# Eight wide warm-up products of TensorE become 32 narrow ones

## The chip, the cores and the metric

The kernel runs on one core of a Trainium2 chip. A core has five engines with instruction streams of their own: TensorE (PE in the profile; PEld is its weight load), VectorE (DVE), ScalarE (ACT), GpSimd (POOL) and SyncE (SP), which here only issues transfers. Engines wait for each other by semaphores. The metric is the device time of one execution in microseconds (us); the median of several runs counts.

## The reference

The kernel computes an attention that picks chunks of keys, then a feed-forward block with a gate. There are 4 sequences with 8 heads, 768 tokens and head size 64. For each query, every chunk of 32 keys gets an upper bound of its score from the chunk's smallest and largest key values; the 6 best chunks (causal) are kept, and softmax attention is done over them alone. The result, 3072 tokens by 512, goes through an RMS norm and the feed-forward block of width 1536.

```python
ub = np.sum(np.maximum(q[:, :, :, None, :] * k_min[:, :, None, :, :],
                       q[:, :, :, None, :] * k_max[:, :, None, :, :]), axis=-1)
...
top_chunks = np.argsort(ub, axis=-1)[..., -top_k:]
scores = scale * np.matmul(q, k.transpose(0, 1, 3, 2))
...
g = xn @ w_gate
silu = g * (1.0 / (1.0 + np.exp(-g)))
val = xn @ w_val
return (silu * val @ w_out).astype(np.float32)
```

## The kernel before

The work is cut into 12 blocks of 256 tokens (a sequence and one of its three parts), in the order of the list `ORDER`. For each block and each group of four heads, DVE transposes keys and queries and reduces the keys to their extremes; TensorE makes the bounds (`upper_first`, line 540, in fp32 for the first part of a sequence; `upper`, line 522, for the others); DVE turns the bounds (tile `ubn`, line 565), takes the best six with a max instruction and makes a mask in two layouts (tiles `mtd` and `mto`, lines 591 and 597). TensorE then makes the scores (line 760) and adds the mask to them in the same accumulation with a product against `chunkrow` (line 771). ACT takes the exponential (tile `pt`, line 810), POOL cuts the triangle on the diagonal, and TensorE multiplies by the values (line 836). After the norm, the feed-forward products stand in line 960 (gate and value) and line 1008 (output); `tanh`, `tg` (line 971), `vs` and `hh` lie between them on ACT, DVE and POOL. Scores go to PSUM tiles called `S`, everything else that TensorE writes to tiles called `F`.

No planner runs at build time. `Plan.STEPS` is a written list: a number from 0 up means operation `x // 8` on engine `x % 8`, and the instructions of each engine stand in the order of this list. `Plan.SLOTS` gives the buffers. A negative number is a step without a result that anyone reads: warm-up products of the identity matrix with itself, written to one of the four `F` tiles, to keep TensorE at work while it waits. `run` (line 227) reads such a number, and `keep_busy` (line 1072) emits the products:

```python
n, slot = divmod(-x, 16)
fill[-1](n // 2, slot, n % 2)
```

So the lowest bit of `n` says whether the products are wide (512 columns, four copies of the identity side by side) or narrow (128 columns), and the rest is their number. Each product has a weight load of its own ahead of it. The first warm-up products of the kernel are 84 narrow ones (the numbers -2368 and -320) while the first transfers are under way; all later ones of before are wide, 38 in all.

In TensorE's program an fp32 product (lines 522 and 540) becomes two loads and two products, every other product one load and one product. With branches and the semaphore waits that stand alone, the program of before has about 9,533 instructions. TensorE's code lies in memory and comes to the engine through a transfer queue of its own during the run.

The two places that the change touches lie early. The first four wide products stand between the scores of the first block's first head group and the bounds of its second (line 540); the second four between the scores of the second head group and the next scores with their mask (lines 760 and 771).

Of the kernel before, what the change touches and what calls it, by code (L numbers as in the profile page):

```python
# [33 lines left out]
class Plan:  # L34
# [13 lines left out]
        131, 228, 233, 123, 155, 3, 99, 249, 244, 27, 257, 276, 291, 34, 281, 268, 299, 83, 412,  # L48
        425, 203, 67, 107, 75, 433, 420, 538, 115, 139, 315, 466, 323, 473, 482, 380, 396, 443, 490,
        545, 42, 498, 404, 307, 522, 388, 529, 506, 594, 515, 179, 611, 562, -2368, -320, 616, 601,  # L50
        554, 672, 626, 681, 571, 50, 457, 578, 786, 587, 634, 689, -82, -82, 792, 642, 57, 650, 699,
        848, 802, 9, 810, 857, 818, 658, 865, 826, 834, 665, 1098, 875, 841, -144, 704, 451, -80,
        736, 912, 713, 746, 922, 754, 1107, 721, 930, 1185, -82, -114, 880, 19, 1042, 731, 331,
        1114, 1049, 1058, 889, 1066, 897, 1130, 1660, 1075, 961, -402, -114, 1248, 1170, 1628, 760,
        1257, 1644, 1082, 1091, 907, 195, 971, 1177, 936, 1684, -80, 1192, 1676, 1362, 977, 1138,
# [1051 lines left out]
```

## Time and profile before

| | |
|---|---|
| median of 3 runs | 293.87 us (292.45 to 294.37) |
| profiled execution | 291.88 us, of which the span is 290.1 us |
| instructions recorded in the span | 11444 |
| busy: TensorE, DVE, ACT, POOL | 96%, 75%, 71%, 58% |
| instruction transfers, queue q8 | 37 packets, 0.61 MB |
| HBM | 28.58 MB read, 6.29 MB written |

Times in the profile count from the start of the span. A busy share is an average over the whole span. "Idle before" names what ended an idle time as far as the profile can tell; "issue" stands where it shows nothing that the engine waited for. Where the engine named had been done long before, something else was waited for. A few records of products are missing (4714 of 4742); the weight loads are complete. The ends of products are modelled, since they overlap.

### The profile page before, as it was taken

Reading aid. Unit: us, or ns where it says so; the run is one execution under the profiler, and the core shown is the slowest. Engines: PE = TensorE matmul, PEld = TensorE weight load, DVE = VectorE, ACT = ScalarE, POOL = GpSimd, SP = SyncE. Lnnn points to the kernel's source line nnn. Section 1 sums busy time; section 2 is a strip of 40 time slices with the busy share of each in tenths; the row PEclk is TensorE's granted clock in tenths of the full one; section 3 lists DMA queues with packets and bytes.
Section 4 is the critical chain, followed back from the end, with each engine's and each line's share of the span. In section 5 each row is a group of like instructions: output and inputs, shape, how many; then the busy total and the mean of one; then the engine's idle time right before and its main releaser. Section 6 shows DMA issues by size and latency. Waiting matters only on the chain.

```text
span 290.1 us, 11444 instructions
## 1 busy us (share of the span) xinstructions
PE 279.4 (96%) x4714; PEld 215.3 (74%) x4742; DVE 216.6 (75%) x626; ACT 206.8 (71%) x355; POOL 167.9 (58%) x268
## 2 busy tenths in 40 slices
PE   7999899999999899999999999999999999999995
PEld 7647897668877667888676787688678966688763
DVE  3878878889898799799989999987573724374341
ACT  2976787678888898877876595877679767564421
POOL 9668779979988785567684485517224207112420
PEclk9999999999999999999999999999999999999999
DMA  9999999989599684468699815912013200303022
GB/s 178 219 194 225 204 211 119 150 160 127 113 165 156 144 155 88 112 99 158 112 178 143 150 25 98 121 12 75 2 20 93 21 3 2 111 18 58 0 91 92
DMA packets 86388, 31.94 MB, mean 110 GB/s; under 512 B 74816, under 2 KB 81728, under 8 KB 86336
## 3 DMA queue, kind: packets, MB, share of 16 engines
q1 hardware_dynamic: 55616, 22.56, 34.0%
q0 software_dynamic: 29712, 7.87, 27.0%
q10 hardware_dynamic: 1008, 0.79, 1.5%
q8 instruction: 37, 0.61, 0.9%
q14 instruction: 15, 0.12, 0.1%
HBM read 28.58 MB, written 6.29 MB: 120 GB/s over the span
## 4 chain that ended last, share of the span: by engine, by line
PE 92%; DVE 3%; issue 2%; DMA 1%; ACT 1%; ACTq 0%; DVEq 0%
PE F L960 44%; PE F L1008 21%; PE S L760 8%; PE F L836 8%; PE S L771 3%; PE F L522 3%; PE F L1075 2%; PE F L540 1%; DMA kraw<-in_k_dram 1%; DVE kx L651 1%; PE F L916 1%; DVE qT L636 0%; DVE kT L636 0%; ACT pt L810 0%; DVE tg L971 0%
## 5 line engine op out<-in xcount | busy, mean ns | idle before, releaser
L810 ACT ACTIVATE pt<-S 128x1024 bf16<-128x1024 f32 (+3 forms) x104 | 85.5, 857 | 29.5 <-PE S L771 26.3
L982 POOL TENSOR_TENSOR hh<-tg,vs 128x512 bf16<-128x512 bf16 x48 | 55.6, 1167 | 45.2 <-DVE tg L971 28.3
L960 PE MATMUL F<-xsT,wg 128*128 128x256 bf16 (+1 forms) x640 | 72.4, 262 | 0.5 <-issue 0.5
L960 PE MATMUL F<-xsT,wv 128*128 128x256 bf16 (+1 forms) x640 | 71.6, 262 | 0.1
L1008 PE MATMUL F<-wo,hh 128*128 128x512 bf16 (+1 forms) x272 | 65.5, 370 | 1.8 <-issue 0.6
L971 DVE SCALAR_TENSOR_TENSOR tg<-th,F 128x512 bf16<-128x512 bf16 x72 | 48.4, 679 | 25.1 <-ACT th L967 19.9
L960 PEld LDWEIGHTS <-wg 128*128 128x128 bf16 x640 | 56.1, 98 | 9.4 <-issue 1.0
L960 PEld LDWEIGHTS <-wv 128*128 128x128 bf16 x640 | 56.1, 98 | 7.7 <-issue 0.2
L967 ACT ACTIVATE th<-F 128x512 bf16<-128x512 f32 x72 | 42.6, 599 | 14.4 <-PE F L960 13.1
L780 POOL TENSOR_SCALAR_AFFINE_SELECT pt<-pt 128x512 bf16<-128x512 bf16 x48 | 31.8, 669 | 27.5 <-ACT pt L810 27.4
L1008 PEld LDWEIGHTS <-hh 128*128 128x128 bf16 x300 | 27.6, 98 | 25.2 <-issue 0.4
L979 ACT ACTIVATE vs<-F 128x512 bf16<-128x512 f32 x48 | 28.5, 599 | 8.9 <-PE F L960 6.0
L760 PE MATMUL S<-qb,kb 32*128 32x256 bf16 (+1 forms) x800 | 33.1, 253 | 0.3 <-issue 0.2
L651 DVE TENSOR_REDUCE kx<-kT 128x16 f32<-128x512 f32 x48 | 31.1, 670 | 0.2
L836 PEld LDWEIGHTS <-pt 128*128 128x128 bf16 x672 | 25.4, 98 | 4.8 <-issue 1.4
L836 PE MATMUL F<-VX,pt 128*128 128x65 bf16 x672 | 27.5, 194 | 1.3 <-issue 1.1
L975 DVE TENSOR_TENSOR hh<-tg,F 128x512 bf16<-128x512 bf16 x24 | 16.1, 682 | 10.2 <-PE F L960 10.0
L760 PEld LDWEIGHTS <-kb 32*128 32x128 bf16 x800 | 13.6, 92 | 13.3 <-issue 11.9
L376 POOL DMA_DIRECT2D VX<-in_v_dram x24 | 22.9, 956 | 0.0
L771 PE MATMUL S<-mto,chunkrow 32*128 32x128 bf16 (+2 forms) x384 | 20.0, 203 | 1.1 <-DVE tg L971 1.0
L771 PE MATMUL S<-mtd,chunkrow 32*128 32x128 bf16 (+2 forms) x384 | 20.3, 203 | 0.0
L771 PEld LDWEIGHTS <-chunkrow 32*128 32x128 bf16 x768 | 18.6, 93 | 2.2 <-issue 1.3
(73 smaller groups left out, 341.2 us busy)
## 6 DMA issues: line engine op xcount, KB each, us to landing
out_dram<-osb SPq DMA_DIRECT2D x23, 256.0 KB, 3.4
kraw<-in_k_dram SPq DMA_DIRECT2D x72, 64.0 KB, 3.3
qraw<-in_q_dram SPq DMA_DIRECT2D x72, 64.0 KB, 3.0
VX<-in_v_dram POOLq DMA_DIRECT2D x24, 128.0 KB, 4.8
QX<-qT SPq DMA_DIRECT2D x32, 64.0 KB, 2.2
wv<-in_moe_w_val_dram POOLq DMA_DIRECT2D x3, 512.0 KB, 11.0
wg<-in_moe_w_gate_dram POOLq DMA_DIRECT2D x3, 512.0 KB, 12.7
wo<-in_moe_w_out_dram POOLq DMA_DIRECT2D x3, 512.0 KB, 9.9
```

Source lines behind the costliest of these rows:

```text
L651: plan.op(f"ext{n}{J}", "DVE", 0.585, 0.67, lambda n=n, op=op: VE.tensor_reduce(out=at(kx)[:, g, n], in_=at(kT).rearrange("p h (j c x) -> ...
L760: TE.matmul(s[a // 2][:, a % 2, c0:c0 + q1 - q0], kbt[r, t, ks], qbt[r, t, q0:q1], start=(t == 0), stop=(t == 1 and not mask), skip_group_ ...
L771: TE.matmul(o, chunkrow[r, BLK * kg + P * e:BLK * kg + P * (e + 1)], mv, start=False, stop=(d == 1), skip_group_check=True)
L780: GE.affine_select(out=d, in_=d, compare_op=ALU.is_ge, fill=0.0, base=0, pattern=[[0, 4], [1, P]], channel_multiplier=-1)
L810: lambda pt=pt, hs=hs, c0=c0, c1=c1, x=sc[hp]: SE.activation(out=at(pt)[:, hs, c0:c1], in_=at(x)[:, :, c0:c1], func=ACT.Exp, scale=SCALE), ...
L836: TE.matmul(o[:, a, :], p_[:, a, off:off + P], vt[:, e, 4 * g + a, :], start=(kb_ == 0 and a == 0), stop=(kb_ == nkb - 1 and a == 3), skip ...
L960: TE.matmul(at(p_)[:, n * W:(n + 1) * W], w[:, g, ht * P:(ht + 1) * P], at(xT)[:, g, x0:x0 + W], start=(g == 0), stop=(g == NP - 1), skip_ ...
L967: plan.op(f"tanh{U}.{hp}", "ACT", 0.48, 0.6, lambda th=th, gp=gp: SE.activation(out=at(th), in_=at(gp), func=ACT.Tanh, scale=0.5), pri - 0 ...
L971: VE.scalar_tensor_tensor(out=at(tg), in0=at(th), scalar=1.0, in1=at(gp), op0=ALU.add, op1=ALU.mult), pri - 30, reads=[th, gp], writes=[tg ...
L979: plan.op(f"vcopy{U}.{hp}", "ACT", 0.48, 0.6, lambda vs=vs, vp=vp: SE.activation(out=at(vs), in_=at(vp), func=ACT.Copy), pri + 0.1, reads= ...
L982: plan.op(f"hh{U}.{hp}", "POOL", 1.11, 1.16, lambda tg=tg, vs=vs, hh=hh: GE.tensor_tensor(out=at(hh), in0=at(tg), in1=at(vs), op=ALU.mult) ...
L1008: TE.matmul(at(op)[:, cs], at(key)[:, o:o + P], wo[:, ht, cs], start=(ht == 0), stop=(ht == NHT - 1), skip_group_check=True)
```

## The change

In `STEPS` two numbers -82 (each two wide products into `F` tile 2) become one number -514 (16 narrow products into the same tile), and -144 (four wide products into `F` tile 0) becomes -512 (16 narrow ones into the same tile). The columns that pass through TensorE are the same: 4 × 512 and 16 × 128. There are 24 more weight loads and 24 more products in TensorE's program, 24 instructions at each place, 48 in all. Everything that stands behind them in the program lies 48 instructions further on. The programs of the other engines are unchanged.

```diff
@@ -48,8 +48,8 @@
         131, 228, 233, 123, 155, 3, 99, 249, 244, 27, 257, 276, 291, 34, 281, 268, 299, 83, 412,
         425, 203, 67, 107, 75, 433, 420, 538, 115, 139, 315, 466, 323, 473, 482, 380, 396, 443, 490,
         545, 42, 498, 404, 307, 522, 388, 529, 506, 594, 515, 179, 611, 562, -2368, -320, 616, 601,
-        554, 672, 626, 681, 571, 50, 457, 578, 786, 587, 634, 689, -82, -82, 792, 642, 57, 650, 699,
-        848, 802, 9, 810, 857, 818, 658, 865, 826, 834, 665, 1098, 875, 841, -144, 704, 451, -80,
+        554, 672, 626, 681, 571, 50, 457, 578, 786, 587, 634, 689, -514, 792, 642, 57, 650, 699,
+        848, 802, 9, 810, 857, 818, 658, 865, 826, 834, 665, 1098, 875, 841, -512, 704, 451, -80,
         736, 912, 713, 746, 922, 754, 1107, 721, 930, 1185, -82, -114, 880, 19, 1042, 731, 331,
```

## The prediction

> **What bounds the kernel now.** I read the page first, then TensorE's waits, then the timeline around the warm-up products, then a table of windows that counts instructions up to chosen moments, and last the instruction queue. From the page:
>
> ```profile
> PE 279.4 (96%) x4714; PEld 215.3 (74%) x4742; DVE 216.6 (75%) x626; ACT 206.8 (71%) x355; POOL 167.9 (58%) x268
> ...
> q8 instruction: 37, 0.61, 0.9%
> ...
> PE 92%; DVE 3%; issue 2%; DMA 1%; ACT 1%; ACTq 0%; DVEq 0%
> ```
>
> TensorE (PE) is busy for 96% of the span and makes up 92% of the chain that ended last. So a time by which it falls behind is lost unless an idle stretch further on gives it back. Its waits:
>
> ```profile
> PE F L836 <- issue: 1.1, 1, 1.1
> PE S L771 <- DVE tg L971: 1.0, 1, 1.0
> PE F L1008 <- issue: 0.6, 4, 0.2
> PE F L960 <- issue: 0.5, 1, 0.5
> PE F L1075 <- DVE ubn L565: 0.3, 1, 0.3
> PE S L760 <- issue: 0.2, 1, 0.2
> ```
>
> Apart from the start these are all of them, 3.7 us. Four (1.1, 1.0, 0.5 and the last 0.2) sit inside groups of like instructions; three of them by the timeline, and a row of DVE:
>
> ```profile
> 15.96 0.28 PE L760 MATMUL S<-qb,kb 32*128 32x128 bf16 x5 [0.20 <-issue]
> ...
> 26.79 0.44 DVE L597 STREAM_TRANSPOSE mto<-mk 64x32 bf16<-64x32 bf16 x2
> ...
> 29.61 0.20 PE L771 MATMUL S<-mto,chunkrow 32*128 32x32 bf16 x4 [1.01 <-DVE tg L971]
> ...
> 99.13 0.70 PE L836 MATMUL F<-VX,pt 128*128 128x65 bf16 x17 [1.10 <-issue]
> ```
>
> The second is put down to DVE's tg, but it reads mto, which DVE had written by 27.23 (26.79 + 0.44), so DVE isn't what it waits for. The idle is counted from the modelled end of the product before; from start to start each is about 0.2 us longer, the length of a short record: 0.4, 1.2, 0.7 (at 36) and 1.3. The windows say where the four lie in the instruction stream (columns: window, length, then busy time and count of PE, PEld, DVE, ACT, POOL, clock, DMA share, GB/s):
>
> ```profile
> 0.00:9.46 9.46, 7.39 (x96) 7.29 (x96) 4.68 (x11) 4.23 (x4) 8.52 (x27) 1.00 1.10 175
> 0.00:13.46 13.46, 11.33 (x195) 9.52 (x199) 8.47 (x30) 8.06 (x14) 10.35 (x32) 1.00 1.12 194
> 0.00:15.90 15.90, 13.63 (x222) 10.63 (x222) 9.83 (x34) 9.80 (x18) 12.79 (x35) 1.00 1.14 199
> 0.00:27.47 27.47, 24.84 (x452) 18.20 (x453) 19.57 (x69) 17.60 (x34) 20.23 (x52) 1.00 1.25 209
> 0.00:29.50 29.50, 25.98 (x477) 19.09 (x477) 21.44 (x74) 19.63 (x38) 22.27 (x55) 1.00 1.22 204
> 0.00:34.31 34.31, 30.68 (x580) 23.64 (x581) 24.96 (x80) 23.21 (x46) 25.45 (x60) 1.00 1.23 204
> 0.00:36.20 36.20, 32.25 (x605) 25.04 (x605) 26.71 (x84) 24.70 (x49) 27.32 (x62) 1.00 1.23 204
> 0.00:41.10 41.10, 36.99 (x706) 29.68 (x706) 31.16 (x91) 28.54 (x56) 30.60 (x70) 1.00 1.23 204
> 0.00:42.35 42.35, 38.24 (x731) 30.89 (x732) 31.98 (x94) 29.79 (x57) 31.85 (x71) 1.00 1.23 205
> 0.00:93.95 93.95, 89.34 (x1483) 69.29 (x1493) 77.07 (x226) 71.50 (x137) 78.01 (x141) 1.00 1.05 171
> 0.00:97.07 97.07, 92.41 (x1586) 71.63 (x1598) 79.86 (x246) 74.58 (x142) 80.48 (x144) 1.00 1.04 171
> 0.00:99.00 99.00, 93.37 (x1613) 72.38 (x1622) 81.35 (x253) 76.45 (x144) 81.46 (x145) 1.00 1.03 170
> ```
>
> Each weight load has one product, so the position is twice the PEld count and the few branches and semaphore waits that the program holds by then (3, 6, 8, 11 or 23). At the four waits it is 222×2+6 = 450, 477×2+8 = 962, 605×2+8 = 1218, 1622×2+23 = 3267: after the first by 512, 768 and 2817, that is, 256 apart to one instruction. They are limits of code blocks, and the whole stream (about 9,533) over the 37 instruction packets gives 258 each. Single packets, by the DMA view of short windows (13.3:13.5, 26.7:26.9, 96.4:96.6):
>
> ```profile
> q8 instruction: 1, 0.02, 34.0%
> q8 instruction: 1, 0.02, 41.8%
> q8 instruction: 1, 0.02, 40.8%
> ```
>
> The first took 34.0% of 16 engines over 0.2 us, 1.09 us, and TensorE resumed at 15.96, 2.6 us after the packet's start; the other two resumed 2.8 and 2.6 us after. The limit before the first stands at 194, which TensorE passed at 9.46 (96×2+3 = 195): so a block seems to be asked for when TensorE enters the one before it, and to start some 4 us later while the DMA share is 1.1 to 1.25. So before 42 us the kernel is held back by its own code, one block per 6 to 7 us.
>
> **The change part by part.** The products themselves:
>
> ```profile
> 7.59 1.78 PE L1075 MATMUL F<-ident 128*128 128x128 bf16 x29
> ...
> 16.38 3.41 PE L1075 MATMUL F<-ident 128*128 128x512 bf16 x15
> ...
> L1075 PE MATMUL F<-ident x122: 219/314/390, 2.1 to 33.7; 128*128 128x128 bf16 x84, 128*128 128x512 bf16 x38
> ```
>
> A row's time holds one record's tail, 0.22 us for a narrow and 0.39 for a wide product. So a narrow one takes (1.78 − 0.22)/28 = 0.056 us and a wide one (3.41 − 0.39)/14 = 0.216. Removed are 8 × 0.216 = 1.73 us, added 32 × 0.056 = 1.78: **+0.06 us**. Their 24 additional weight loads run beside the products, as in the row of 29. Nothing moves on another engine, no wait is added and no DMA.
>
> What moves is the code limits. Both places stand after instruction 194 and before 450, so the limits up to 194 stay, and every later one (450, 706, ...) falls on work that was 48 instructions earlier: 402, 658, 914, 1170, 1426, ..., 3218 of before.
>
> *Limit 450.* The block is asked for at instruction 194, ahead of the change, so its packet starts at 13.3 to 13.5 as now and TensorE can go on at 15.96. It gets to the 402 of before at 13.46 (199×2+6 = 404), now 13.52, and stands for 15.96 − 13.52 = **2.44 us** where it lost 0.4. From there 48 instructions of work, 2.1 us with its seven wide warm-up products, are still to be done that were behind it: it is 15.96 − 13.46 − 0.4 = 2.1 us late. None of this is cover for another wait: DVE and ACT wait for TensorE soon after, and warm-up products are a fixed list that a late TensorE still executes.
>
> *Limit 706* (658): no idle now, and TensorE comes 2.1 us later to it, so none.
>
> *Limit 962* (914). TensorE comes at 27.47 + 2.1 = 29.6. If the packet starts in 26.7:26.9 as now, the block is there at 29.6: the 1.2 us of idle there (28.4 to 29.6) is gone but for 0.1. But instruction 657 of before waits for DVE's ubn (the row of 0.3 us), and the block is asked for at 658, now right behind that wait, which itself comes 2.1 us later; then I count up to 0.8 us. *Limit 1218* (1170): TensorE comes at 34.31 + 2.1 − 1.2 + (0.1 to 0.8) = 35.3 to 36.0, the block at 36.36 + (0 to 0.8), so 1.1 us where 0.7 is lost now. *Limit 1474* (1426): now TensorE shows no wait there, and by the same count it and the block come within 0.1 of each other; I take 0.1 now and then.
>
> The early sum: 0.06 + 2.44 + (0.1 to 0.8) + 1.1 + 0.1 = 3.8 to 4.5, less 0.4 + 1.2 + 0.7 + 0.1 = 2.4 now: +1.4 to +2.1. From the other side: as long as the blocks set the pace, they come at the same times and TensorE is 48 instructions short at each; at 1474 that is the time from 41.10 to 42.35, 1.2 us. So +1.2 to +2.1; I take **+1.8**, near the upper end, since the wait for ubn is a row and stands where the request does.
>
> *Limit 3266* (3218). It costs 1.3 us now. TensorE passes the limit before it, 3010 (1493×2+23 = 3009), at 93.95, and the packet starts at 96.4:96.6, late for this part, behind a load of SP:
>
> ```profile
> 93.25 0.40 SPq L376 DMA_DIRECT2D gB<-in_moe_rms_g_dram  x1
> ```
>
> With the limit at 2962 the request goes out sooner; I can't read from the trace how far ahead of the products the sequencer asks. The quick instructions between 2962 and 3010 take 0.4 us, and the slower products of L960 before them up to 2 us for the same count; so the request is 0.4 to 2 us sooner, an estimate. TensorE needs the block 99.13 − 97.07 less the idle of 1.3 = 0.8 us sooner. So the idle becomes 0.1 to 1.7; if the packet's start does not move at all, 2.1. An earlier request also comes ahead of the 256 KB of gB. I take 0.4, near the lower end for that, which is **−0.9**, with −1.3 and +0.8 as ends.
>
> *The 32 other limits* show no such row (the longest issue wait left is 0.2 us); I take 0, with +0.8 as an end, one new idle of the middle size.
>
> Sum: 1.8 − 0.9 + 0 = **+0.9 us**. The profiled execution took 291.88 us (span 290.1), so 292.8 of its kind; it lies 2.0 under the median of the runs, 293.87, which gives **294.8 us**.
>
> The Trainium skill ("Runtime: NRT & Kernel Launch", Instruction fetch mechanics) has blocks of 256 instructions fetched by the sequencer itself, and calls the cost of crossing a limit mostly hidden. The trace agrees with the 256 and not, in this kernel, with the second; by it alone the sum would be the 0.06 us of the products.
>
> **The rivals.** *Not slower: the late limit pays for the early ones.* The request for 3218 gets ahead of gB and its idle goes but for 0.1 (−1.2), while the request for 914 isn't held by ubn and the early debt is the 1.2 of limit 1474: 0.0, so 293.9. It decides from an early debt below what 3266 gives back. For it: 1.2 us is the bound that the pace gives. Against it: the ubn row.
>
> *The limits don't matter.* The waits would be something else and the products alone count: 293.9. Against it are four idle times that lie 256 apart to the instruction, one of them, at 99.13, ahead of the last 17 of a run of L836 products.
>
> *No gain at 3266.* The packet waits out the same transfers: +0.8 instead of −0.9, with +2.1 early: +2.9, 296.8, and 297.6 with one new idle of 0.8.
>
> *The clock falls.* The first products ran slowly:
>
> ```profile
> 2.07 5.19 PE L1075 MATMUL F<-ident 128*128 128x128 bf16 x47 [2.07 <-POOL ident masks.py:199]
> ```
>
> That is 0.11 us each against 0.056 later: half speed for some 5 us. If an idle of 2.4 us sends TensorE back to it for as long, half of 5.2 is lost: +2.6 on the 0.9, 297.4. Against it: idles of 1.2 us left every window at 1.00 clock. The Trainium skill ("TensorE: Matmul & The Clock Gate", The HAM clock gate) asks for an idle window of about 3.4 us before the clock is halved; 2.4 is below it, and no run shown here has one so long.
>
> **How the numbers follow.** My forecast, early debt with part of it given back, 0.58; late limit pays for all 0.18; limits don't matter 0.03; no gain at 3266 0.15; clock 0.06. About 1% (2.9 us) is what a measurement of this kernel can tell from no change. The forecast and the first two rivals stay within it, but for 0.05 each way for a gap of the early fetches that opens or closes more than I count; the last two lie at or over it. So faster 0.05, same 0.75, slower 0.20. The range goes from the early debt 1.2, 3266 at −1.3 and the runs' own spread below the median (293.87 − 292.45 = 1.4) to the third rival with an idle more: 292.5 to 297.5.
>
> **What would show it.** TensorE idle from about 13.5 to 16 in a group of L771 with an issue wait of some 2.4 us: the central step. Then the DVE tg wait of 1.0 us at 29.6 gone or smaller and moved to the start of an L960 group; an idle near 36 of about 1.1; the issue wait at 98 smaller or gone; all counted positions of these waits again at 450 + 256k. The clock in 15:25 stays 1.00. I'm wrong if the first packet starts sooner than 13.3, if early limits show idles whose sum isn't 3.8 to 4.5, or if a late limit opens a new one.

## The result and the profile after

The kernel after the change took 293.84 us (median; 292.52 to 295.97) beside 292.51 us for the kernel before in the same session, a ratio of 1.0048 with a 95% interval of 1.0027 to 1.0069. It is 1.3 us slower: less than the 1% that the prediction took as the least that counts as a change, but clear of no difference, since the interval doesn't reach 1. The forecast had been +0.9. In absolute terms it had been 294.8 us, 1.0 too high, because it started from a median of three runs (293.87) that lies 1.4 above the one of 22 here, while the difference itself was 0.4 too small.

The execution of after that was profiled is one of its slowest (295.97 us, span 294.2). From its page:

```profile
PE 281.5 (96%) x4738; PEld 216.9 (74%) x4766; DVE 216.9 (74%) x626; ACT 206.7 (70%) x355; POOL 167.8 (57%) x268
...
PEclk9979999999999999999999999999999999999999
...
q8 instruction: 37, 0.61, 0.9%
```

There are 24 more weight loads and still 37 instruction packets. New is the 7 in the third slice of the clock row: TensorE did not have its full clock all the time. TensorE's waits (us in total, times, longest), without the wait for ident at the start and one of 0.3 us for ubn that before has too:

```profile
PE S L771 <- issue: 2.0, 1, 2.0
PE F L960 <- DMA xsT<-xs: 0.9, 1, 0.9
PE F L836 <- DVE tg L971: 0.8, 1, 0.8
PE F L1008 <- issue: 0.6, 4, 0.2
PE F L960 <- DVE tg L971: 0.4, 1, 0.4
PE F L836 <- DVE hh L975: 0.4, 1, 0.4
PE F L540 <- DVE BO L676: 0.4, 1, 0.4
```

Of before's four waits at block limits (0.2, 1.0, 0.5 and 1.1 us) none is left. In their place stands one, larger and early. Five rows are of waits that before did not have: one for BO, early, and four for xsT, tg (two) and hh, all after 113 us. The timeline around the large one:

```profile
14.46 0.18 PE L771 MATMUL S<-mtd,chunkrow 32*128 32x32 bf16 x2
16.59 0.19 PE L771 MATMUL S<-mtd,chunkrow 32*128 32x32 bf16 x2 [1.95 <-issue]
...
17.48 2.33 PE L1075 MATMUL F<-ident 128*128 128x512 bf16 x5
```

TensorE stops after the second of four products of a group, at instruction 450 of its program, which is where the prediction put it. Between the starts of the weight loads on its two sides the idle is 2.18 us, against 0.42 before. The last row is what was not forecast: five wide products take 2.33 us, where in before fifteen took 3.41 us, 0.216 each. The table of windows (window, length, then busy time and count of PE, PEld, DVE, ACT, POOL, granted clock, DMA share, GB/s) has the clock beside it:

```profile
17.36:20.77 3.41, 3.41 (x46) 1.47 (x43) 3.24 (x8) 2.21 (x5) 1.36 (x2) 0.50 1.57 195
13.95:17.36 3.41, 1.42 (x42) 0.91 (x41) 0.85 (x2) 1.28 (x6) 2.48 (x4) 1.00 1.36 217
```

For 3.41 us the clock is 0.50, and in the 3.41 us ahead of that TensorE was busy for only 1.42.

I followed where the time went by matching the weight loads of the two profiled executions in order and taking the difference of their starts. After is 3.1 us behind at the work of before's 13.46 (of it 2.2 at the limit; 0.9 came in ahead of it, with the data of the first products), 4.2 behind at 19.7, within the slow stretch, 2.7 at 29.6, 2.0 at 36.4, 0.9 at 99.1: the idles of before at limits 962, 1218 and 3266, which are missing here, give back 1.2, 0.7 and 1.2. Then it loses again: 1.9 behind at 113.5, 3.6 at 129.4, and 4.1 at the end. This execution lies 2.1 us above the median of its kernel and that of before 0.6 below its own; so the profiles differ by three times what the medians do, and more profiles were needed.

### The profile page after: what moved, and what is told of

Its sections match the earlier page's. It is cut to its first block, busy times and chain, and to the rows that moved or that the text cites. A ratio compares the mean times of both kernels' runs of the same rounds, so it can differ in the third digit from the quotient of the medians.

```text
span 294.2 us, 11492 instructions
## 1 busy us (share of the span) xinstructions
PE 281.5 (96%) x4738; PEld 216.9 (74%) x4766; DVE 216.9 (74%) x626; ACT 206.7 (70%) x355; POOL 167.8 (57%) x268
## 4 chain that ended last, share of the span: by engine, by line
PE 80%; DMA 7%; DVE 5%; SPq 3%; issue 3%; ACT 1%; ACTq 0%; DVEq 0%
PE F L960 39%; PE F L1008 17%; PE S L760 7%; PE F L836 6%; PE F L1075 3%; DMA qraw<-in_q_dram 3%; SPq L376 3%; PE S L771 2%; PE F L522 2%; PE F L540 1%; DMA out_dram<-osb 1%; DMA kraw<-in_k_dram 1%; DMA xsT<-xs 1%; DVE xs L890 1%; DVE qT L636 1%
## 5 line engine op out<-in xcount | busy, mean ns | idle before, releaser
L780 POOL TENSOR_SCALAR_AFFINE_SELECT pt<-pt 128x512 bf16<-128x512 bf16 x48 | 31.1, 654 | 29.4 <-ACT pt L810 29.1
L1075 PE MATMUL F<-ident 128*128 128x128 bf16 (+1 forms) x146 | 18.4, 292 | 2.4 <-POOL ident masks.py:199 2.1
```

The costliest lines, as they stand in the source:

```text
L780: GE.affine_select(out=d, in_=d, compare_op=ALU.is_ge, fill=0.0, base=0, pattern=[[0, 4], [1, P]], channel_multiplier=-1)
```

## The experiments

Times are medians beside the kernel before in the same session, with the ratio and its 95% interval. "From start to start" is the idle of a limit measured between the starts of the weight loads on its two sides, so that a limit without idle has about 0.05. The position of a limit is named by its instruction in TensorE's program (450, 706, 962, ...).

**1. The first of the two places alone**, a shift of 24 instead of 48.

```diff
- ... 634, 689, -82, -82, 792, 642, ...
+ ... 634, 689, -514, 792, 642, ...
```

> Only the first of the two places is changed: four wide products become 16 narrow ones, and the code limits from 450 on fall on work that stood 24 instructions earlier (426, 682, 938, 1194, ..., 3242 of before). Theory of the limits: the first idle lies between the one of before (0.4 us) and the one of the changed kernel (2.2 us), about 1.7 us, ends near 16, and stands at instruction 450 of the program; the idle at 3266 shrinks from 1.3 to about 0.8. Rival (narrow products cost by themselves): half of what the whole change costs, +0.7 us, and the waits where they were before. Theory of the clock: an idle of 1.7 us halves TensorE's clock in fewer executions than one of 2.2 us.

293.69 us beside 292.64, ratio 1.0036 (1.0003 to 1.0069). The idle at 450 is 1.67 us from start to start, as the halved shift asks. That the size fits so well is partly luck, since both sides of it were late in this execution: the packet started at 14.62 instead of 13.38, and TensorE was 1.3 us late on its way to the limit, 0.9 of it in a wait for BO. The idle has moved to another group, 24 instructions of work from where 48 put it:

```profile
15.72 0.29 PE L836 MATMUL F<-VX,pt 128*128 128x65 bf16 x4
17.47 0.30 PE L836 MATMUL F<-VX,pt 128*128 128x65 bf16 x4 [1.45 <-POOL mhalf L394]
```

It is put down to POOL's mhalf here and to "issue" in after: the name changes with the group, the position in the program doesn't. At 3266 0.27 us is left of 1.29 (I had expected 0.8). The clock is 0.50 from 17.72 to 21.13 here too; of the 12 executions 2 have a mean clock below 0.9965, against 9 of 22 of after. So the second set of narrow products is not needed for the idle, and its place goes with the position of the limit.

**2. The limits put back**: after, with 32 of the narrow products of the kernel's start made eight wide ones. The changed places stay narrow, 48 instructions fewer stand ahead of instruction 194, and all limits from 450 on fall on the same work as before.

```diff
- ... 562, -2368, -320, 616, ...
+ ... 562, -1344, -272, -320, 616, ...
```

> The change as it is, and 32 of the 84 narrow products at the start become 8 wide ones, which takes the 48 instructions out again ahead of limit 194. The limits from 450 on fall on the same work as before the change; the limit at 194 falls on work that stood 48 instructions later. Theory of the limits: idle times again at the places of before (962: 1.2, 1218: 0.7, 3266: 1.3 us). If the block of 450 is asked for when TensorE enters 194, the first idle is 0.8 to 2.0 us instead of 0.4, since 194 is entered 1.6 us later; if it is asked for at a fixed time, 0.4. Rival (the narrow products cost by themselves): the time of the changed kernel, +1.3 us, with the waits of before.

292.84 us beside 292.64, ratio 1.0005 (0.9979 to 1.0030): the loss is gone with the narrow products still in place. The waits of before are back, as at 962:

```profile
29.53 0.18 PE L771 MATMUL S<-mtd,chunkrow 32*128 32x32 bf16 x4
30.61 0.19 PE L771 MATMUL S<-mto,chunkrow 32*128 32x32 bf16 x4 [0.89 <-DVE tg L971]
```

From start to start 1.11 us at 962, 1.06 at 3266. So narrow products in those two places cost nothing by themselves. This run can't tell the limits from a cost of every instruction in the program, since it has as many narrow products in all as before; experiment 3 comes back to that. Two details missed: no idle at 1218 (0.7 expected), and one of 0.09 at 450 where I had expected 0.8 to 2.0. Limit 194 was passed 1.4 us later than in before, but the packet for 450 started only 0.6 us later (14.02 instead of 13.38). So the packet is not simply a fixed time behind the passing of the limit ahead of it: over the thirteen profiles the packet for 450 started 3.0 to 4.4 us behind it.

**3. A wide start**, in before: all 84 narrow products of the start become 21 wide ones, 126 instructions fewer ahead of limit 194.

```diff
- ... 562, -2368, -320, 616, ...
+ ... 562, -592, -112, 616, ...
```

> Before, with all 84 narrow products of the start as 21 wide ones: 126 instructions fewer, the two later places as before. The limits move the other way: 450 falls on work of instruction 576 of before, and is asked for later. Theory of the limits: no idle at 450 at all (needed at 19.9, there at about 18), one of about 1.4 us at the third limit near 30, none or little after; 1.5 us less idle than before, 291.0 us. Rival (the first products or the sum of columns decide): as before, since the columns are the same.

291.20 us beside 292.64, ratio 0.9954 (0.9919 to 0.9989). Its waits hold no limit at all any more:

```profile
PE F L960 <- DVE tg L971: 0.4, 1, 0.4
PE F L960 <- DMA xsT<-xs: 0.3, 1, 0.3
PE F L1075 <- DVE ubn L565: 0.3, 1, 0.3
PE F L836 <- DVE ubn L565: 0.2, 1, 0.2
```

I had expected 1.4 us at the limit near 30, so that detail missed. Along the shared work TensorE is 1.6 us ahead of before at 29.6, 3.5 at 99 and 2.4 at the end.

The medians of all experiments rise with the number of instructions (126 fewer, 78 fewer, as many, 24 more, 48 more), so a small cost of every instruction would fit them nearly as well as the limits. The traces speak against it. Such a cost would show where the instructions are, at the start; but TensorE is only 0.1 us ahead at 19.7. Its lead comes in steps at the places of before's waits, 1.2 us at 962, 0.7 at 1218 and 1.3 at 3266, and stays within 0.2 us between these steps.

**4. The same wide start in after.**

> The changed kernel with the same wide start: 78 instructions fewer than before. Theory of the limits: no idle at 450, one of about 0.9 us near 30, 1.7 us less idle than before, 290.8 us, although the 32 narrow products of the change are all there; and the clock stays at full in all executions, since no idle reaches 2 us. Rival (the narrow products cost by themselves): 1.3 us over the run with the wide start alone.

292.25 us beside 292.64, ratio 0.9984 (0.9949 to 1.0020). I had expected 290.8 us, so this one missed. There is no idle at 450, as expected, but at 962 it is 1.6 us where I had expected 0.9:

```profile
29.40 0.26 PE L836 MATMUL F<-VX,pt 128*128 128x65 bf16 x3
31.04 0.34 PE L836 MATMUL F<-VX,pt 128*128 128x65 bf16 x5 [1.38 <-issue]
```

With 78 instructions fewer instead of 126 the limits fall less well. Beside experiment 3 (292.25 and 291.20 in the same session) the change costs about 1.0 us here too, but the two intervals overlap, so this is not clear of noise. I had also expected a full clock in every execution, since no idle reaches 2 us. But 4 of 12 have a mean clock below 0.9965, as do 4 of 12 in experiment 3, whose profile shows no idle at a limit.

**5. After once more**, for a second profile.

> The changed kernel once more, for a profile in which TensorE's clock is not halved and for the share of executions in which it is. Theory of the clock: the idle of 2 us at 450 is there in each execution; where the clock stays full, the run is about 293.3 us, 0.6 over before, and TensorE's delay at 36 us (work of instruction 1218) is about 0.2 to 1 us instead of 2.0. Rival (the clock has no part in it): the same delays as in the profile with the halved clock.

293.83 us beside 292.36, ratio 1.0050 (1.0015 to 1.0085): the difference holds. The second profile is unlike the first. Here data came late, and TensorE waited for them ahead of limit 450; the row of waits, and the windows around it:

```profile
PE F L540 <- DVE BO L676: 1.5, 1, 1.5
...
8.00:10.00 2.00, 0.49 (x15) 0.32 (x12) 0.95 (x3) 0.59 (x2) 1.01 (x4) 1.00 1.44 191
...
11.98:15.39 3.41, 3.41 (x61) 2.84 (x58) 2.91 (x16) 2.79 (x10) 1.86 (x4) 0.50 1.18 258
```

The clock fell to a half for 3.41 us after that wait, before the limit was reached. TensorE came to 450 late for both reasons and stood only 0.86 us; 0.41 at 962, 0.62 at 1218, none at 3266. It is 1.3 us behind before at 36.4, 0.2 at 99 and 1.4 at the end. In 8 of the 10 executions the mean clock is below 0.9965; their median is 293.90 us, that of the two others 293.18.

**6. The late limits alone**: in before, 8 of the 15 wide products at 16.4 become 32 narrow, so that limits 194 and 450 stay and those from 706 on shift by 48. If the early idle at 450 is the loss and 3266 the gain, this version has the gain alone.

```diff
- ... 1075, 961, -402, -114, 1248, ...
+ ... 1075, 961, -242, -1026, 1248, ...
```

> Before, with the first two places as they were; of the 15 wide warm-up products at 16.4 us eight become 32 narrow ones. The same 48 instructions more, but after limit 450: the first limit stays where it was, all from 706 on shift as in the changed kernel. Theory of the limits: the idle at 450 is 0.4 us as before, the one at 3266 is gone, those at 962 and 1218 come to about 2.3 us together (1.9 before); 0.7 us less idle than before, 291.9 us, and the clock is halved as rarely as before. Rival (48 instructions or 32 narrow products cost by themselves, wherever they stand): the time of the changed kernel, +1.3 us.

293.50 us beside 292.36, ratio 1.0038 (1.0004 to 1.0072); I had expected 291.9, so this one missed, and the time is the one that the rival gave (48 instructions or 32 narrow products cost wherever they stand: +1.3). The limits did nearly as expected: idle 0 at 450 (0.4 expected), 1.2 at 962, 1.2 at 1218, 0.05 at 3266, and TensorE is 0.7 us ahead of before at 99. So the trace shows no cost of the products or the instructions up to there, and the rival's number does not come about in the rival's way. But TensorE is 0.9 behind at 112.7 and 3.1 at 129.4. From its timeline at 27 to 36 and 113 to 133:

```profile
28.39 0.84 PE L960 MATMUL F<-xsT,wg 128*128 128x128 bf16 x12 [0.95 <-issue]
...
35.13 0.90 PE L960 MATMUL F<-xsT,wv 128*128 128x128 bf16 x13 [0.90 <-issue]
...
113.59 1.05 PE L836 MATMUL F<-VX,pt 128*128 128x65 bf16 x28 [1.60 <-DVE ubn L565]
...
129.56 1.03 PE L960 MATMUL F<-xsT,wg 128*128 128x256 bf16 x8 [0.40 <-DVE tg L971]
131.35 0.80 PE L836 MATMUL F<-VX,pt 128*128 128x65 bf16 x20 [0.75 <-DVE tg L971]
132.54 0.92 PE L836 MATMUL F<-VX,pt 128*128 128x65 bf16 x24 [0.40 <-DVE hh L975]
```

The last three rows are the same three waits, with the same lengths, as in after, and experiment 1 has them too (0.55, 0.75, 0.39). My reading was that TensorE hands to DVE what it gains at 3266; experiments 8 to 10 test it. Why the row of 1.60 us for ubn is there, no run shows.

**7. The wide start once more.**

> Before with the 84 narrow products of the start as 21 wide ones, once more, to narrow its interval: by the theory of the limits again 1 to 2 us under before, 291 us; by the rival (the first result was luck of the executions) 292.6.

291.62 us beside 292.36, ratio 0.9959 (0.9922 to 0.9996). Again no limit stands in its waits; TensorE is 3.6 us ahead at 99 and 1.1 at the end, with 2.0 us lost to xsT. 3 of 12 executions have a mean clock below 0.9965.

**8 to 10. The copy at 127 us moved from DVE to ACT**, in after, in before and in the wide start. The three waits at 130 to 133 follow a stretch in which DVE's copy into QX takes long. DVE and POOL in after:

```profile
127.81 1.62 DVE L692 COPY QX<-qT 128x512 f32<-128x512 f32 x1
129.35 0.67 DVE L971 SCALAR_TENSOR_TENSOR tg<-th,F 128x512 bf16<-128x512 bf16 x1
...
127.31 1.58 POOL L982 TENSOR_TENSOR hh<-tg,vs 128x512 bf16<-128x512 bf16 x1
```

and in before:

```profile
124.96 0.85 DVE L692 COPY QX<-qT 128x512 f32<-128x512 f32 x1
...
125.51 1.32 POOL L982 TENSOR_TENSOR hh<-tg,vs 128x512 bf16<-128x512 bf16 x1
```

In after the copy takes 1.62 us and shares 1.1 us of it with POOL's product; in before it takes 0.85 us, of which 0.3 lie beside that product. That the product makes it slow was a guess: POOL was busy with other work beside most of the rest of the copy in both. One number of `STEPS` puts it on ACT:

```diff
- ... 9968, 5730, 9777, ...
+ ... 9968, 5729, 9777, ...
```

> The changed kernel with one copy into QX (line 692, at 127.8 us in its profile, where it takes 1.62 us on DVE beside a product of POOL; 0.85 in before) moved to ACT. Theory that the gain at 3266 is given back to DVE, which falls behind between 105 and 131 us: TensorE's waits near 130 (0.4, 0.8 and 0.4 us, put down to DVE's tg and hh) shrink by about 1 us, and the kernel comes to 0.5 to 1 us under the changed one, 292.9 to 293.4. Rival (DVE has nothing to do with it; the limits or the clock alone make the difference): as the changed kernel, 293.8.

> Before with the same copy on ACT. TensorE has no wait near 130 there, so by the theory nothing is to be had: within 0.4 us of before. Rival (the copy on DVE costs in each kernel): 0.5 to 1 us under before.

> The wide start with the same copy on ACT. Its profiles lose 0.3 and 1.3 us to waits between 113 and 131 us, in part to DVE: 0 to 0.5 us under the wide start alone, 290.9 to 291.4; by the rival as the wide start, 291.4.

After with it: 293.94 us beside 292.11, ratio 1.0063 (1.0034 to 1.0093). Before with it: 292.85, 1.0039 (1.0007 to 1.0070). Wide start with it: 291.04, 0.9974 (0.9945 to 1.0003). Where I expected a gain of 0.5 to 1 us in after, there is none, the wide start gains nothing beside its two other sessions either, and before rather loses. Between after and before, both with the copy on ACT, lie 1.1 us, so the loss of the change is there in this pair too. In the profile of 8 the waits for tg and hh are down to one of 0.5 us (a new one of 0.4 is put down to ACT's pt), and the time did not follow. So those waits, in after's first profile, do not explain its median, and the reading that DVE takes back the gain is not borne out.

The profile of 8 served for something else. Its TensorE program is that of after, and the execution kept its clock:

```profile
17.00:21.00 4.00, 4.00 (x50) 1.83 (x48) 4.00 (x10) 2.77 (x6) 2.33 (x7) 1.00 1.54 192
```

Here the limits can be read undisturbed (timeline, TensorE; two rows for each of 450, 962 and 1218):

```profile
13.70 0.18 PE L771 MATMUL S<-mtd,chunkrow 32*128 32x32 bf16 x2
15.46 0.19 PE L771 MATMUL S<-mtd,chunkrow 32*128 32x32 bf16 x2 [1.58 <-issue]
...
28.51 0.39 PE L960 MATMUL F<-xsT,wg 128*128 128x128 bf16 x4
29.87 0.84 PE L960 MATMUL F<-xsT,wg 128*128 128x128 bf16 x12 [0.97 <-issue]
...
35.38 0.33 PE L960 MATMUL F<-xsT,wv 128*128 128x128 bf16 x3
36.34 0.90 PE L960 MATMUL F<-xsT,wv 128*128 128x128 bf16 x13 [0.63 <-issue]
```

From start to start 1.81, 1.24 and 0.90 us, with 0.33 at 1474: 4.28 in all, where before has 0.42, 1.23, 0.74 and 0.13, 2.52. The difference is 1.76, and past the limit 1474 TensorE is indeed 1.8 us later than in before; it is 0.5 later at 99.1 and 1.8 at the end.

The profile of 9 has the early program of before, and its clock fell: the packet for 962 came late, the idle there is 2.1 us, and a stretch of 3.41 us at half clock follows.

```profile
28.85:32.26 3.41, 1.55 (x52) 1.39 (x52) 1.54 (x3) 1.44 (x4) 2.29 (x5) 1.00 1.15 187
32.26:35.67 3.41, 3.41 (x40) 3.41 (x38) 2.89 (x6) 2.17 (x4) 1.90 (x3) 0.50 1.23 208
```

**11. Before once more**, for a second profile of it.

> The kernel before, unchanged, profiled a second time. Ratio 1.000 by every theory; what is asked is the profile. Theory: the 1 to 3.7 us that TensorE loses between 99 and 131 us in the profiles of the changed kernels, to waits for xsT, tg and hh, are not the change's but a chance of single executions, and the profile of before that all were compared with has none of them by luck. Then this profile shows such waits too, 0.7 to 3 us in all, and TensorE ends 0.5 to 3 us later along the shared work than in the first profile of before. Rival: a shift of the limits brings them, by way of the order in which the engines meet there. Then this profile has no wait over 0.4 us between 99 and 131 us and ends within 0.5 us of the first. By both the idle times at 450, 962, 1218 and 3266 are about 0.4, 1.2, 0.7 and 1.3 us as before.

292.46 us beside 293.43 for the same kernel, ratio 0.9986 (0.9950 to 1.0021). Its waits:

```profile
PE S L771 <- DVE tg L971: 0.9, 1, 0.9
PE F L836 <- issue: 0.9, 1, 0.9
PE F L960 <- issue: 0.7, 1, 0.7
PE F L960 <- DMA xsT<-xs: 0.6, 1, 0.6
```

The limits are as in the first profile (1.1 us at 962, 1.0 at 1218, 1.1 at 3266) but for 450, which has no idle this time. The profile lies between the two expectations: a wait for xsT comes up in before, too, by chance, but only 0.6 us, and the waits for tg and hh do not.

## Why the prediction was right, and where not

*The mechanism stands up to 99 us; the number is in part luck.* The limits 48 instructions further on make the early idle and take away the late one: experiment 2 takes the shift back, keeps the narrow products in their places, and the early idle and the loss are gone. With it falls the rival that the limits don't matter. At 99.1 us, when all the limits of the sum are past, TensorE is behind the first profile of before by 0.85, 0.22 and 0.48 us in the three profiles of the changed program; the forecast for this point was +0.9. The rest of their delay, 1.2 to 3.2 us, comes later, where the sum had nothing. So the measured +1.3 is not simply the forecast sum come true.

*Products, +0.06.* Nothing in the runs is against it: experiment 2 has the narrow products in both changed places, and before's time, and experiment 6 has 32 of them elsewhere and is ahead of before at 99 us.

*First idle, 2.44.* Right in kind and place. The profiles of the changed program have 2.18, 0.86 and 1.81 us. The packet starts at 13.86 in after; this is the instruction queue in 13.8:14.0:

```profile
q8 instruction: 1, 0.02, 36.3%
```

I had taken 13.3 to 13.5, and products resuming 2.6 us later; they resumed 2.5 to 2.7 later in the three. But TensorE came to the limit later than I reckoned in two of the three, because the data for its first products moved by up to 1.5 us from one execution to the next. A wait ahead of a limit comes off the idle at it. The packet started at 12.97 in the profile of experiment 8, which by the prediction was a sign of being wrong (sooner than 13.3); it started at 12.85 in the second profile of before too, so the start was taken as more fixed than it is.

*Limits 962 to 1474.* The sum of the early idles, 3.8 to 4.5, was met in the profile with a full clock (4.28, and an early debt of 1.8 as taken). That is partly luck, since its terms lay elsewhere and cancelled: 1.81 at 450 for 2.44, 1.24 at 962 for 0.1 to 0.8, 0.90 at 1218 for 1.1, 0.33 at 1474 for 0.1. In the two profiles with a halved clock TensorE is behind the packets anyway, and the early idles sum to 2.3 and 2.0; there the prediction's test "sum 3.8 to 4.5" fails. The limits still stand where it put them.

*Limit 3266, −0.9.* Mis-sized: there is no idle left in any profile of the changed program (0.05 from start to start), so it gives back 1.2. The packet starts at 95.05 in after, 0.7 us before TensorE's products pass the limit ahead of it, where in before it started 2.5 behind; I had allowed for 0.4 to 2 us sooner, and it came 3.2 sooner by that measure. The rival "late limit pays for all" was right about this limit, and wrong about the early ones. "No gain at 3266" is refuted. With 1.2 instead of 0.9 my sum is +0.6.

*The other 32 limits, 0.* In after they show no new idle, as taken.

*The clock.* This step failed: the clock was to stay full, with a chance of 0.06 that it doesn't, because a single idle of 2.4 us seemed too short. The Trainium skill ("TensorE: Matmul & The Clock Gate", The HAM clock gate) gives a window of about 3.4 us, which I took as a time that has to be idle throughout. The trace agrees with the length: each slow stretch lasts 3.41 us. It does not agree with my reading, since TensorE had been busy for 1.42 us of the stretch ahead in after and 1.90 of it in experiment 1:

```profile
14.31:17.72 3.41, 1.90 (x45) 1.11 (x44) 1.31 (x5) 2.37 (x8) 3.27 (x6) 1.00 1.38 213
17.72:21.13 3.41, 3.41 (x41) 1.35 (x38) 3.33 (x8) 1.69 (x3) 0.72 (x2) 0.50 1.56 192
```

The traces also suggest why the clock falls in some executions only. After the opening the clock was full from 7.11 to 17.35 in after, from 7.47 to 17.71 in experiment 1, from 5.15 to 11.98 in experiment 5 and from 4.95 to 32.26 in the profile of 9: three, three, two and eight times 3.41 us. So it seems to be settled anew every 3.41 us, at moments that differ from one execution to the next, by how busy TensorE was since the last one. In the profile of 8 such a moment, at 14.38, falls into the idle at 450 and shares it out:

```profile
10.97:14.38 3.41, 2.85 (x89) 2.25 (x86) 2.85 (x16) 2.84 (x10) 2.34 (x4) 1.00 1.19 259
14.38:17.79 3.41, 2.33 (x50) 1.29 (x53) 1.42 (x5) 1.40 (x3) 2.19 (x5) 1.00 1.46 207
```

The four stretches ahead of a half clock have TensorE busy for 1.42, 1.55, 1.90 and 2.00 us; three others with 1.81 to 1.89 (in 1, 6 and 9, after 110 us) were not followed by one. So the limit lies somewhere there, and these runs don't fix it.

A mean clock below 0.9965 was recorded in 23 of 43 executions of the changed program (9 of 22, 8 of 10, and 6 of 11 in experiment 8) and in 18 of the 105 of before that stood beside the experiments. What that costs stays open. In after such executions have a median of 294.70 us, the others 293.27; but in experiment 8 the two are 294.00 and 293.94, and slow stretches come with idles that cost time themselves. By medians alone, 1.4 us in 24% more executions would be 0.3 of the 1.3. The full-clock executions of before have 292.41 over all sessions (291.87 to 292.63 in single ones), 0.9 below the full-clock ones of after. No run here changes the clock and nothing else.

*After 99 us, nothing.* I had taken TensorE's delay to reach the end unchanged. It does not: between 99 and the end after's profile loses 3.2 us more, its second profile 1.2, experiment 6 3.7, experiment 3 1.1, before's second profile 0.6. Most of it goes to waits for xsT, tg, hh or ubn, that is, to DVE and its transfers. Experiments 8 to 10 took away one suspected cause, the copy beside POOL, and won nothing. One part comes by chance: at the work of before's 113.5, where after waits for xsT, the three profiles of the changed program lose 0.9, 0.8 and 0.5 us, and the second profile of before loses 0.65, while its first loses none. What the rest is stays open; the three waits of 0.40, 0.75 and 0.40 stand in the profiles of after, 1 and 6 and not in the second one of after, so they are not a fixed price of the shift either. That the whole loss belongs to the change rests on the repeated ratios (1.0048 and 1.0050, and 1.0063 with the copy on ACT), not on a trace.

*The range.* From its own terms it comes out as 292.4 to 297.6 instead of 292.5 to 297.5. It is 5 us wide and reaches down to the time of before, so that the result lies in it says little. The chance of 0.75 for no change is 0.69 by its own terms, unless part of the third rival, which lies at the bound, is counted in.

The version that beats both kernels is the wide start without the change: 0.9954 and 0.9959 of before in two sessions.

## What to carry to other kernels

Before changing the number of instructions early in a program, count at which instruction its code blocks end and how far ahead of its work each block arrives: here 48 instructions more, with the same work, cost 1.3 us, and 126 fewer won 1.4 and 0.7 us between medians in two sessions. Idle times whose attribution changes from group to group, but which lie a fixed number of instructions apart, can be limits of code, and fewer instructions for the same warm-up time make them come later in the work. A change that takes an idle away doesn't have to win its length: the three profiles of the changed program were 0.2 to 0.9 us behind at 99 us, past the limits that counted, and lost 1.2 to 3.2 us more after that. Where the bounding engine hurries, look at which engine it then meets, and take more than one profile before giving a late wait to the change.

## What the runs showed of the hardware that was not expected

- The TensorE clock was granted at 0.50 for 3.41 us after stretches of 3.41 us in which TensorE had been busy for 1.42 to 2.00 us, with a single idle of 1.7 to 2.2 us in them or, in experiment 5, most of one of 1.5 us for data. In the execution of experiment 8 an idle of 1.81 us, shared by two such stretches, was not followed by it.
- The start of the packet for the same block differs by over 1 us between executions: the one for limit 962 started at 26.83 and 26.51 in the two profiles of before, and at 28.03 in that of experiment 9, whose early program is the same. There the idle at 962 is 2.1 us instead of 1.2:

```profile
PE S L771 <- DVE tg L971: 1.9, 1, 1.9
```

- The same copy on DVE (128x512 f32) took 0.85 us in one execution and 1.62 in another, with 0.3 and 1.1 us of it beside a POOL product; the cause is not shown.
